# Pooled attention and a top-1 mixture of experts on one core: the last pair's sums earlier, the routings' products and the first expert's weight pieces in other places, the gates on ScalarE

## The chip, the core and the metric

The kernel runs on one core of a Trainium2 chip. Five engines work beside each other, each on its own queue in order: TensorE (PE; its weight loads are listed as PEld), VectorE (DVE), ScalarE (ACT), GpSimd (POOL) and SyncE (SP), which here only issues transfers. The metric is the device time of one execution in microseconds. About 2% is what a measurement of this kernel can tell from no change.

## The reference

K and V are averaged over 8 neighbouring rows, softmax attention is taken over the 72 pooled rows, and each of the 4608 resulting rows of 512 goes to one of 8 experts, the one with the largest logit.

```python
k_p = k.reshape(B, H, Sp, pool, D).mean(axis=3)      # B = H = 8, S = 576, D = 64, Sp = 72
v_p = v.reshape(B, H, Sp, pool, D).mean(axis=3)
attn = softmax(scale * q @ k_p.T)
x = (attn @ v_p).transpose(0, 2, 1, 3).reshape(4608, 512)
expert_idx, gate_w = argmax(x @ w_gate), softmax(x @ w_gate)[expert_idx]
# each expert takes its rows in order, up to capacity (1152); rows beyond it give zero
h = np.maximum(np.einsum('ecd,edf->ecf', disp, w1), 0.0)   # F = 1024
y = np.einsum('ecf,efd->ecd', h, w2)
out[i] = gate_w[i] * y[expert_idx[i], pos[i]]
```

## The kernel before

Attention runs over 36 *units*. A unit is 256 rows of one batch for four heads, and each odd batch is led by a unit for the last 64 rows of two batches. The main loop (`for n in range(nu + 2)`, from L1022) works on unit n's scores (`score`, PE writes ps), its row maxima and differences on VectorE (`softmax`: mx at L486, pt at L491), and its exponentials on ScalarE (`exp`, L494), while PE transposes unit n-2 (`p_t`, pp, copied to pT by ScalarE at L503), multiplies it by the pooled V (`av`, pa, L516) and VectorE normalises it (`norm`: rz, reciprocal, xo, lt, L525 to L542). There is one tile pa, so PE's next `av` waits until `norm` has read it, that is until lt. `q_part` transposes the next unit's queries (pq), which ScalarE copies to qT (L463). Small products and transposes share two PSUM banks in turn (`bank`).

Around this stand queues of small pieces, taken a few at a time by `step`: gq (GpSimd's sums for pooling, `tree`: three additions a third, L370 to L374; later the pieces of w1), rq (the routings), dq (the masks) and sq (scatters of routed rows to `slots`, L679, each behind a small write of the tile `apart`). `load_kv` brings the raw K and V of a pair of batches, `pool` sums them: that of the fourth pair (batches 6 and 7) is put on the queue at the end of unit 14, behind a copy that waits for unit 14's mx.

A *routing* (`route`) is a chain of some 18 VectorE operations on the logits of two batches: gmx, gd, gme, gmm, the one-hot rows oh, their running sums su, the counts (L628), then on PE the products po, and behind them gps (a sum, and a product with oh), gpos, ghi, gix and pairs. Each `yield` in it is one step. It stands in rq from units 10, 19 and 28 on, and for batch 6 from 32; `step(rq)` is called once in `softmax`, three times in `norm` and once ahead of `norm`, there with 4 steps, or 8 in the last eight units. `favourite` finds from the second routing which expert leads, and its w1 is loaded (L816) and split into two halves of precision in eight pieces (`split_early`): ScalarE copies w1h (L125), GpSimd subtracts w1l (L126).

After attention a loop runs over tiles of 256 rows of one expert. PE makes the hidden rows (ph, three banks, L150), ScalarE takes relu into hh (L1129), VectorE the rest into hl (L1130), PE multiplies by w2 (y, L159). Where the expert changes (`sw`), ScalarE and VectorE split w1 and w2 (w2h at L125, w2l at L126). `gate` scales y into ys (L1152), GpSimd scatters ys and rows of zeros to the output (L100) and gathers the next rows (xg, L95). Ahead of a pass each engine loads registers from the table cf (L1159 to L1165).

Of the kernel before, what the change touches and what calls it, by code (L numbers as in the profile page):

```python
# [10 lines left out]
F32 = mybir.dt.float32  # L11
# [20 lines left out]
def pooled_attn_top1_moe(ctx: ExitStack, tc: tile.TileContext, q, k, v, wg, w1, w2, cap, out):  # L32
# [7 lines left out]
    nc = tc.nc  # L40
# [121 lines left out]
    with ExitStack() as actx:  # L162
# [421 lines left out]
        def route(bp, t0, G, blk, tail, prods, sc, count=False, run=None):  # L584
# [43 lines left out]
                    nc.vector.tensor_reduce(out=cum[-1], in_=oh[:, NB : 4 * NB + 2].bitcast(F32).rearrange("p f e -> p e f"), axis=AX.X, op=ALU.add)  # L628
                yield
            if gn > 3:  # L630
                yield
                yield
                yield
            po = bank([P, 512], "po")[:, 0 : 4 * E].rearrange("p (a e) -> p a e", a=4)
            prods = [x for x in prods if before or x[1] != "c"]
            for n_, (w, x, l, m) in enumerate(prods):
# [98 lines left out]
        def drain(q_):  # L735
            while q_:
                step(q_)

        with tc.manual_schedule():
# [17 lines left out]
            def ahead(b):  # L757

                if b + 1 < B:
                    load_q(b + 1)  # L760
                if b % 2 == 0:
                    load_qtail(b)
                if b == LAST - 1:
                    dq.append(masks)

            nu = len(units)
# [238 lines left out]
            def hooks(n):  # L1005

                p, j = divmod(n, NPU)
                if n == 0:
                    red(vps[0][:, NR - 1 :], raws[0][1][2][:, 2:3])
                    pooled(1)  # L1010
                    pool(1)
                if p == B // 2:
                    return
                if p + 2 < B // 2:
                    if j == (4 if p == 0 else 2):
                        load_kv(p + 2)
                    if j == (7 if p == 0 else 5):
                        if p:
                            nc.gpsimd.tensor_copy(apart, early["mx"][:, 0, 0:1])
                        pooled(p + 2)  # L1020
                        pool(p + 2)
                if n == 3 * NB:  # L1022
                    drain(gq)
                    gq.append(setup_rest())
                    drain(gq)
                    setup_rows()

            for n in range(nu + 2):
                u = units[n] if n < nu else None
                p = units[n - 2] if n > 1 else None  # L1030
                nx = units[n + 1] if n + 1 < nu else None
                new = n and u and u.b != units[n - 1].b
                if new:
                    assert not aq
                    ahead(u.b)
                if n == n_start:
                    start_weights()
                if n == n_early:
                    start_early()
                if n == n_early + 1:  # L1040
                    drain(gq)
                    split_early(0, 2 * KD, nc.gpsimd)
                if n == n_early + 3:
                    start_ids()
                if n == n_early + 4:
                    start_rows()
                if u:
                    u.score(0)
                if p:
                    p.p_t(0)  # L1050
                if u:
                    u.score(1)
                    u.softmax()
                step(aq)
                if p:
                    p.p_t(1)
                if n == nu + 1:
                    for c in range(KF):
                        nc.scalar.copy(wr["h"][:, c], wr[2][:, c])
                if n >= nu:  # L1060
                    hidden(0, n - nu)
                if nx:
                    nx.q_part()
                flush()
                step(aq)
                if n == 1:
                    busy(5)
                    hq.append(prep_v(0))
                    step(hq)
                if u:  # L1070
                    u.exp()
                if p:
                    p.open()
                    p.av(0)
                turns(n)
                if p:
                    p.av(1)
                step(rq, 4 if NPU < n < nu - 8 else 8 if n >= nu - 8 else 0)
                step(dq)
                if p:  # L1080
                    p.norm()
                    r = route_of(p)
                    if r:
                        rq.append(r)
                        if p.b == early_b - 1:
                            rq.append(favourite())
                hooks(n)
                step(gq, 4 if n <= n_early else 0 if n_early + 3 <= n < n_early + 5 else 2)
                step(sq, 2 if n < nu - 10 else 4)
                step(aq)  # L1090
            flush()
# [4 lines left out]
    with ExitStack() as bctx:  # L1096
# [52 lines left out]
                split(hh[s], hl[s], p)  # L1149

        def gate(i):
            nc.vector.tensor_scalar_mul(ys[i], y[i], io[:, i, 1:2].bitcast(F32))  # L1152

        nc.sync.dma_start(xs[NT : NT + 1, :], zrow[0:1])
        nt = nc.values_load(ntl[0:1, 0:1], min_val=E, max_val=MT // 2 + E)
# [1 line left out]
        with tc.For_i(0, nt, 1, iteration_sync="reg_based") as t:  # L1157
            with tc.manual_schedule():
# [24 lines left out]
                load_w1(we, cond=nw > 0, bounds_check="skip_entire_dma")  # L1183
                columns(io[:, :, 1], ids[:, ds(ct, 2), 1])
                masked(io[:, :, 0], ct, mkeep)
                gate(1)
                masked(iz, cd, mdrop)
                nc.gpsimd.tensor_sub(guard[:, 0], iz, iz)
                for i in range(2):
                    scatter(iz[:, i : i + 1], zrow[:, :], across_iterations=True)  # L1190
                gate(0)
                with tc.If(sw > 0):
                    split_w2()
                load_w2(we, cond=nw > 0, bounds_check="skip_entire_dma")
                for i in (1, 0):
                    nc.gpsimd.tensor_sub(guardf, ys[i][:, 0:2], ys[i][:, 0:2])
# [27 lines left out]
```

## Time and profile before

| | us |
|---|---|
| median of 3 runs | 640.29 (633.51 to 642.54) |
| the profiled execution | 639.53 |
| its span, first to last instruction | 637.5 |
| PE busy in it | 614.1 (96%) |
| DVE, ACT, POOL busy | 332.5, 236.3, 297.4 |
| mean granted PE clock | 0.987 |

The views of the profile that are read below: busy time and clock by stretch, the waits summed by pair, the timeline of one engine, and the chain of work that ended last. In a timeline a row gives the start and the length in us, the engine, the line of the program, the operation, out<-in, the form, the count, and in brackets how long the engine was idle before and what ended that. Units begin on PE at 64.27 (unit 11), 68.72 (12), 75.13 (13), 108.95 (21), 145.45 (28), 150.17 (29), 162.87 (31) and 179.07 (34).

### The profile page before, as it was taken

How to read it: one execution, taken by the hardware profiler on the slowest of the kernel's cores; microseconds unless marked ns; L12 is line 12 of the kernel's file. 1: busy time of each engine (PE TensorE's matmuls, PEld its weight loads, DVE VectorE, ACT ScalarE, POOL GpSimd, SP SyncE). 2: the span in 40 equal slices, each digit the busy share in tenths (PEclk: the TensorE clock that was granted, in tenths of full speed). 3: DMA queues.
4: the chain of work that ended last, by engine and by line, in shares of the span. 5: the costliest groups of instructions: out<-in, count | busy, mean ns of one | idle time of the engine just before them, and what ended most of it. 6: DMA issues, size and time to landing. Idle time of an engine off the chain costs nothing.

```text
span 637.5 us, 14824 instructions
## 1 busy us (share of the span) xinstructions
PE 614.1 (96%) x4249; PEld 554.1 (87%) x4250; DVE 332.5 (52%) x720; ACT 236.3 (37%) x403; POOL 297.4 (47%) x468
## 2 busy tenths in 40 slices
PE   9899999899999999999899999999999999999994
PEld 8889899798889889988789989988899888989983
DVE  4667868777788322268447731326422585323222
ACT  2555576366544211157245511117111472111111
POOL 7799499253743422424435522434434145441344
PEclk9999999799999999999999999999999999999997
DMA  9989953283191610228728640213612181210112
GB/s 325 359 330 323 349 183 122 72 258 101 53 329 53 230 35 33 66 81 309 241 82 308 230 141 33 66 33 120 235 47 66 41 282 36 66 51 19 62 49 66
DMA packets 47084, 93.81 MB, mean 147 GB/s; under 512 B 13392, under 2 KB 23632, under 8 KB 47060
## 3 DMA queue, kind: packets, MB, share of 16 engines
q1 hardware_dynamic: 30836, 60.37, 27.6%
q0 software_dynamic: 11392, 21.57, 11.3%
q10 hardware_dynamic: 4832, 11.56, 4.8%
q8 instruction: 14, 0.23, 0.1%
q14 instruction: 10, 0.08, 0.0%
HBM read 132.97 MB, written 31.27 MB: 258 GB/s over the span
## 4 chain that ended last, share of the span: by engine, by line
PE 60%; DVEq 2%; issue 2%; DVE 1%; POOL 1%; ACT 0%; POOLq 0%; ACTq 0%
PE y L159 30%; PE ph L150 23%; PE ph L1140 4%; PE px L1117 2%; PE ph L1147 1%; DVE w2l L126 0%; POOL out_dram L100 0%; DVE hl L1130 0%; DVEq L1165 0%; DVEq L1164 0%; DVEq L1163 0%; ACT w2h L125 0%; DVEq L1160 0%; DVEq L1159 0%; POOL xg L95 0%
## 5 line engine op out<-in xcount | busy, mean ns | idle before, releaser
L1129 ACT ACTIVATE hh<-ph 128x512 fp32r<-128x512 f32 x60 | 35.8, 598 | 170.1 <-PE ph L150 170.0
L1130 DVE SCALAR_TENSOR_TENSOR hl<-ph,hh 128x512 fp32r<-128x512 f32 x60 | 40.7, 690 | 109.4 <-ACT hh L1129 62.5
L150 PE MATMUL ph<-xh,w1h 128*128 128x256 f32 x480 | 76.5, 282 | 4.6 <-DVE hl L1130 3.9
L150 PE MATMUL ph<-xh,w1l 128*128 128x256 f32 x480 | 75.9, 281 | 0.0
L150 PE MATMUL ph<-xl,w1h 128*128 128x256 f32 x480 | 75.9, 281 | 0.0
L150 PEld LDWEIGHTS ph<-xh,w1h 128*128 128x128 f32 x480 | 65.8, 189 | 6.9 <-DVE hl L1130 4.8
L159 PE MATMUL y<-w2h,hh 128*128 128x512 f32 x280 | 71.7, 398 | 0.0
L95 POOL DMA_INDIRECT xg<-xs,ix x42 | 43.5, 1035 | 58.2 <-PE y L159 50.0
L516 PE MATMUL pa<-vbd,pT 96*128 96x146 f32 (+1 forms) x480 | 67.1, 296 | 3.5 <-DVE lt L542 3.5
L159 PE MATMUL y<-w2h,hl 128*128 128x512 f32 x280 | 69.3, 390 | 0.0
L159 PE MATMUL y<-w2l,hh 128*128 128x512 f32 x280 | 69.2, 389 | 0.0
L150 PEld LDWEIGHTS ph<-xl,w1h 128*128 128x128 f32 x480 | 65.2, 190 | 0.0
L150 PEld LDWEIGHTS ph<-xh,w1l 128*128 128x128 f32 x480 | 64.7, 189 | 0.0
L516 PEld LDWEIGHTS pa<-vbd,pT 96*128 96x128 f32 (+1 forms) x480 | 57.1, 181 | 6.8 <-DVE lt L542 4.5
L159 PEld LDWEIGHTS y<-w2l,hh 128*128 128x128 f32 x280 | 52.6, 188 | 11.1
L159 PEld LDWEIGHTS y<-w2h,hl 128*128 128x128 f32 x280 | 52.6, 188 | 10.9
L100 POOL DMA_INDIRECT out_dram<-zrow,iz x40 | 51.3, 1282 | 16.9 <-issue 14.9
L159 PEld LDWEIGHTS y<-w2h,hh 128*128 128x128 f32 x280 | 49.6, 188 | 9.6 <-ACT hh L125 0.9
L126 DVE TENSOR_TENSOR xl<-px,xh 128x512 fp32r<-128x512 f32 x40 | 25.8, 686 | 60.9 <-ACT xh L125 60.9
L93 POOL TENSOR_TENSOR guard<-ix 128x2 int32<-128x2 int32 x21 | 4.0, 193 | 101.5 <-DVE ix L90 96.8
L503 ACT COPY pT<-pp 96x384 f32<-96x384 f32 x72 | 33.8, 474 | 45.0 <-PE pp L502 44.4
L679 POOL DMA_INDIRECT slots<-pairs,gix x36 | 35.4, 983 | 30.3 <-DVE pairs L672 13.0
(236 smaller groups left out, 1051.8 us busy)
## 6 DMA issues: line engine op xcount, KB each, us to landing
r<-in_moe_w_dram SPq DMA_DIRECT2D x84, 1024.0 KB, 11.1
raw<-in_k_dram SPq DMA_DIRECT2D x12, 768.0 KB, 6.5
raw<-in_v_dram SPq DMA_DIRECT2D x12, 768.0 KB, 10.6
xs<-xo ACTq DMA_DIRECT2D x16, 512.0 KB, 3.1
qblk<-in_q_dram SPq DMA_DIRECT2D x14, 512.0 KB, 7.7
raw<-in_moe_w_dram SPq DMA_DIRECT2D x4, 512.0 KB, 4.8
r<-in_moe_w_dram ACTq DMA_DIRECT2D x2, 1024.0 KB, 6.9
qblk<-in_q_dram SPq DMA_DIRECT2D x4, 256.0 KB, 8.3
```

Source lines behind the costliest of these rows:

```text
L95: nc.gpsimd.indirect_dma_start(out=dst[:, i, :].bitcast(F32), out_offset=None, in_=src, in_offset=bass.IndirectOffsetOnAxis(ap=ix[:, i, 0: ...
L100: ins = nc.gpsimd.indirect_dma_start(out=out[:, :], out_offset=bass.IndirectOffsetOnAxis(ap=i_, axis=0), in_=src, in_offset=None, bounds_c ...
L126: eng.tensor_sub(lo, src, hi.bitcast(F32))
L150: nc.tensor.matmul(p[:, f2], a[:, c, f * P : (f + 1) * P], b[:, c], start=(f2 == 0 and j == 0 and c == 0), stop=(f2 == 1 and j == 2 and c ...
L159: nc.tensor.matmul(y, a[:, c, i * P : (i + 1) * P], b[:, c], start=(n == 0), stop=(n == 3 * KF - 1))
L503: nc.scalar.copy(self.pT[:, j], pp[0:KC, 0:HC])
L516: nc.tensor.matmul(self.pa[us, j, h0 * XW : (h0 + 2) * XW], self.pT[:, j, c, us], vbd[b % 2][:, cc].rearrange("r a x -> r (a x)"), start=( ...
L679: ins = nc.gpsimd.indirect_dma_start(out=slots[:, :], out_offset=bass.IndirectOffsetOnAxis(ap=ix[:, g, 0:1], axis=0), in_=pairs[:, pr + g0 ...
L1117: nc.tensor.transpose(px[i][:, c], xg[:, i, c * P : (c + 1) * P], identr)
L1129: nc.scalar.activation(hh[s], p, AF.Relu)
L1130: nc.vector.scalar_tensor_tensor(out=hl[s], in0=p, scalar=0.0, in1=hh[s].bitcast(F32), op0=ALU.max, op1=ALU.subtract)
L1140: nc.tensor.matmul(ph[f], a[:, c, r], b[:, c, fs], start=(j == 0 and c == 0), stop=(j == 2 and c == KD - 1))
```

## The change

Six edits:

- In `route`, the chains of more than three tiles take 5 (with counts) or 7 (without) empty steps ahead of the products po, where there were 3.
- `step(rq)` ahead of `norm` takes 8 steps in all units below 14 (before: 4 from unit 10 on), then 4, and 8 in the last eight as before.
- The fourth pair's sums are put on the queue at the end of unit 12 instead of unit 14, behind a copy that waits for unit 12's mx; three steps of gq follow in that unit, so one K sum stands ahead of the first scatters.
- The eight pieces of w1 are taken 2, 3, 3 at units 26, 27 and 28 (before: 2, 2 at 26 and 27, and 2, 2 at 30 and 31); the additional ones stand behind `p_t(0)` and `p_t(1)`.
- The masks are made at unit 22 instead of 27.
- `gate` is an ACTIVATE on ScalarE with a scale from io, and both gates stand behind the split of w2.

```diff
             if gn > 3:
-                yield
-                yield
-                yield
+                for _ in range(5 if count else 7):
+                    yield
...
-                if b == LAST - 1:
+                if b == LAST - 2:
                     dq.append(masks)
...
-                    if j == (7 if p == 0 else 5):
-                        if p:
-                            nc.gpsimd.tensor_copy(apart, early["mx"][:, 0, 0:1])
+                    if p == 0 and j == 7:
                         pooled(p + 2)
                         pool(p + 2)
                 if n == 3 * NB:
...
+                    nc.gpsimd.tensor_copy(apart, early["mx"][:, 0, 0:1])
                     setup_rows()
+                    pooled(3)
+                    pool(3)
...
+                more = 1 if n_early + 1 < n < n_early + 4 else 0
                 if u:
                     u.score(0)
                 if p:
                     p.p_t(0)
+                step(gq, more)
...
                 if p:
                     p.p_t(1)
+                step(gq, more)
...
-                step(rq, 4 if NPU < n < nu - 8 else 8 if n >= nu - 8 else 0)
+                step(rq, 8 if n < 2 * NPU - 4 or n >= nu - 8 else 4)
...
-                step(gq, 4 if n <= n_early else 0 if n_early + 3 <= n < n_early + 5 else 2)
+                step(gq, 3 if n == 3 * NB else 4 if n <= n_early else 2 if n == n_early + 1 else 1)
...
         def gate(i):
-            nc.vector.tensor_scalar_mul(ys[i], y[i], io[:, i, 1:2].bitcast(F32))
+            nc.scalar.activation(ys[i], y[i], AF.Copy, scale=io[:, i, 1:2].bitcast(F32))
...
-                gate(1)
                 masked(iz, cd, mdrop)
...
-                gate(0)
                 with tc.If(sw > 0):
                     split_w2()
+                for i in (1, 0):
+                    gate(i)
```

On GpSimd, behind the last piece of `setup_rest` (rmi, unit 12), the order before is this; slots are the scatters, t and kp the tiles of a sum:

```order
L335 IOTA rmi_187 32x64
L678 MEMSET apart_184 128x1
L679 DMA slots_64<-pairs_66,gix_1120 36864x2
L678 MEMSET apart_184 128x1
L679 DMA slots_64<-pairs_66,gix_1120 36864x2
L1019 COPY apart_184<-mx_1168 128x1
L370 TENSOR_TENSOR t1_1211<-raw_1001 128x768
```

and in the changed kernel:

```order
L335 IOTA rmi_187 32x64
L1023 COPY apart_184<-mx_1026 128x1
L370 TENSOR_TENSOR t1_1106<-raw_1001 128x768
L372 TENSOR_TENSOR t2_1107<-t1_1106 128x384
L374 TENSOR_TENSOR kp_1104<-t2_1107 128x192
L677 MEMSET apart_184 128x1
L678 DMA slots_64<-pairs_66,gix_1080 36864x2
```

The copy waits for unit 12's mx instead of unit 14's, and the first K sum moved ahead of the first two scatters.

On VectorE, in the same unit 12, behind PE's products po of the first routing, there stood before:

```order
L644 TENSOR_TENSOR gps<-su,po 128x64
L646 SCALAR_TENSOR_TENSOR gps<-po,oh_180 128x8
L655 TENSOR_TENSOR gps<-gps,oh_180 128x64
L525 TENSOR_SCALAR rz<-pa 128x8
L658 TENSOR_REDUCE gpos<-gps 128x9
L527 RECIPROCAL rz<-rz 128x8
L662 TENSOR_SCALAR ghi<-gpos 128x9
L541 TENSOR_TENSOR xo<-pa,rz 128x2x256
L542 TENSOR_TENSOR lt<-pa,rz 128x2x32
```

and now stands:

```order
L643 TENSOR_TENSOR gps<-su,po 128x64
L645 SCALAR_TENSOR_TENSOR gps<-po,oh_180 128x8
L654 TENSOR_TENSOR gps<-gps,oh_180 128x64
L657 TENSOR_REDUCE gpos<-gps 128x9
L661 TENSOR_SCALAR ghi<-gpos 128x9
L663 TENSOR_SCALAR ghi<-ghi 128x9
L664 SCALAR_TENSOR_TENSOR gpos<-gpos,gmm 128x9
L667 TENSOR_REDUCE gse<-ex_183 128x9
L669 SCALAR_TENSOR_TENSOR gix<-ghi,gpos 128x9
L671 RECIPROCAL pairs<-gse 128x9
L525 TENSOR_SCALAR rz<-pa 128x8
```

The rest of the chain moved ahead of the normalisation rz, xo, lt of unit 10.

On ScalarE, from the exponential of unit 27 to the first pT of unit 29, there stood before (in the changed kernel the two pieces ahead of the exponential of unit 27 come on top):

```order
L494 ACTIVATE pt<-pt 128x576
L125 CAST w1h<-raw 128x512 x2
L503 COPY pT<-pp 96x384 x2
L463 COPY qT<-pq 128x512
L494 ACTIVATE pt<-pt 128x576
L417 COPY kbs_147<-pk 64x64x5
```

and now stands:

```order
L494 ACTIVATE pt<-pt 128x576
L125 CAST w1h<-raw 128x512
L503 COPY pT<-pp 96x384
L125 CAST w1h<-raw 128x512
L503 COPY pT<-pp 96x384
L125 CAST w1h<-raw 128x512
L463 COPY qT<-pq 128x512
L494 ACTIVATE pt<-pt 128x576
L417 COPY kbs_147<-pk 64x64x5
L417 COPY kbs_147<-pk 64x64x4
L417 COPY kbs_147<-pk 64x64x5
L417 COPY kbs_147<-pk 64x64x4
```

Pieces of w1 (w1h) moved between the copies pT, and one more, the eighth, follows these kbs copies ahead of unit 29's first pT.

## Rows read from the trace of the kernel before

**Rows 1.** Busy time and granted clock (PEclk) by stretch, us.

```profile
105.00:135.00 30.00, 27.86 (x218) 24.78 (x217) 24.23 (x74) 15.19 (x31) 13.92 (x20) 0.89 0.45 158
150.00:165.00 15.00, 14.29 (x111) 12.83 (x110) 10.73 (x33) 7.84 (x17) 4.27 (x5) 0.89 0.24 72
```

**Rows 2.** Timeline of PE: waits at the routings, and places named.

```profile
71.39 1.02 PE L516 MATMUL pa<-vbd,pT 96*128 96x146 f32 x6 [0.41 <-DVE lt L542]
...
77.68 1.66 PE L516 MATMUL pa<-vbd,pT 96*128 96x146 f32 x12
...
113.34 1.01 PE L516 MATMUL pa<-vbd,pT 96*128 96x146 f32 x6 [2.13 <-DVE lt L542]
...
147.53 0.66 PE L462 MATMUL pq<-identr,qblk 128*128 128x128 f32 x4 [0.28 <-ACT pT L503]
...
155.28 0.28 PE L641 MATMUL po<-su,matr 128*128 128x16 f32 x1 [0.71 <-DVE su L621]
...
166.34 1.01 PE L516 MATMUL pa<-vbd,pT 96*128 96x146 f32 x6 [0.75 <-DVE lt L542]
...
178.94 0.27 PE L641 MATMUL po<-su,matr 128*128 128x8 f32 x1 [1.19 <-DVE su L621]
...
184.38 1.74 PE L516 MATMUL pa<-vbd,pT 96*128 96x146 f32 x12
```

**Rows 3.** Timeline of DVE: second routing (two rows) and third.

```profile
107.83 1.59 DVE L598 TENSOR_TENSOR gd<-lg,gmx 128x72 f32<-128x72 f32 x1
...
109.98 1.69 DVE L614 TENSOR_TENSOR oh<-cw,gmm 128x64 fp32r<-128x64 f32 x1
...
153.49 0.22 DVE L598 TENSOR_TENSOR gd<-lg,gmx 128x72 f32<-128x72 f32 x1
```

**Rows 4.** Timeline of POOL: fourth pair's sums, first and last tree.

```profile
82.56 1.83 POOL L370 TENSOR_TENSOR t<-raw 128x768 f32<-128x768 f32 x1
...
107.51 1.81 POOL L370 TENSOR_TENSOR t<-raw 128x768 f32<-128x768 f32 x1
```

**Rows 5.** Timeline of DVE: units 11 and 12, and a routing's chain undivided.

```profile
71.26 0.34 DVE L628 TENSOR_REDUCE oh<-oh 128x8 fp32r<-128x112 f32 x1
71.52 0.75 DVE L486 TENSOR_REDUCE mx<-ps 128x8 f32<-128x576 f32 x1
...
75.49 0.22 DVE L655 TENSOR_TENSOR gps<-gps,oh 128x64 f32<-128x64 f32 x1
...
76.73 0.21 DVE L542 TENSOR_TENSOR lt<-pa,rz 128x64 f32<-128x64 f32 x1
...
197.69 0.17 DVE L644 TENSOR_TENSOR gps<-su,po 128x16 f32<-128x16 f32 x1 [0.92 <-PE po L641]
...
198.89 0.18 DVE L672 RECIPROCAL pairs<-gse 128x3 f32<-128x3 f32 x1
```

**Rows 6.** Timelines of DVE, POOL and ACT: ghi, pieces of w1, copies kbs.

```profile
163.32 1.11 DVE L662 TENSOR_SCALAR ghi<-gpos 128x9 f32<-128x9 f32 x1
...
161.88 2.49 POOL L126 TENSOR_TENSOR w1l<-raw,w1h 128x512 fp32r<-128x512 f32 x2 [9.83 <-ACT w1h L125]
...
145.98 1.12 ACT L125 CAST w1h<-raw 128x512 fp32r<-128x512 f32 x2
...
149.44 1.72 ACT L417 COPY kbs<-pk 64x320 f32<-64x320 f32 x4
```

**Rows 7.** PE's waits summed; ACT's timeline; the chain that ended last.

```profile
PE ph L150 <- DVE hl L1130: 3.9, 4, 1.8
...
524.81 2.00 ACT L125 CAST w2h<-r 128x1024 fp32r<-128x1024 f32 x2 [0.55 <-DMA r<-in_moe_w_dram]
...
239.07 11.31 PE ph L150 x96
...
526.93 0.07 DVEq L1192
...
531.17 0.70 DVE hl L1130
```

## The prediction

> **What bounds the kernel.** I read the busy time and granted clock by stage first, then TensorE's waits, then the orders of the engines around each wait. TensorE (PE) works almost without a pause, so a term counts only where PE waits, or works at the lower clock, and where nothing else comes to wait there instead. In the attention stage such places lie at the four routings. [...] Behind the third routing PE waits 0.75 us (unit 31), behind the fourth 1.19 us (unit 33) [rows 2]. In the expert loop the only waits that repeat are those for hl where an expert changes: 3.9 us in four places [rows 7].
>
> **Second routing (sums moved to unit 12).** The wait of 2.13 us comes from VectorE: gd took 1.59 us and oh 1.69 us there, where the same gd of the third routing took 0.22 us [rows 3]. gd ended at 109.42; GpSimd's first step of the last V sum, begun at 107.51 and 1.81 us long, ended at 109.32 [rows 3, 4]. So these operations, which read two SBUF operands, stood until GpSimd's sum was through. The fourth pair's sums ran from 82.56 to the tree begun at 107.51 [rows 4]. Now they are issued behind unit 12's mx, which begins at 71.52 and takes 0.75 us [rows 5]: a start at 72.6, 10 us sooner. Even with two more slot scatters between them they are over well ahead of 107. gd and oh then take some 0.2 us, lt ends about 0.4 us before PE needs it, and PE waits for nothing: -2.13 us. If the fall of the clock hangs on that wait, 3.3 us come back too: together -5.4.
>
> **First routing (eight steps a unit instead of four; K sum beside it).** What was spread over units 11 to 13 now stands ahead of two normalisations. In unit 11 the counts (0.34 us, L628) move ahead of lt [rows 5], and PE already waited 0.41 us for that lt at 71.39 [rows 2]: +0.35. In unit 12 everything from gpos to pairs moves ahead of rz. A whole such chain, with nothing between, took from 197.69 to 198.89 plus 0.18 [rows 5]; its part behind gps and the product is 0.95 us. The K sum's last step overlaps its start: begun at 72.6, its steps of 1.83 us [rows 4] and, at half and a quarter of the size, about 1.0 and 0.6 us end near 76.3, and the product, at 75.49 before [rows 5], would be due at 75.9; I add 0.3 us. lt, at 76.73 plus 0.21 before, ends at 76.94 + 0.35 + 0.95 + 0.3 = 78.55, and PE's pa of unit 13, begun at 77.68 before [rows 2], is due at 78.05: a new wait of 0.5, with the hand-over 0.65. Below, the chain meets no sum (+0.3); above, one operation stands behind a whole first step of 1.83 us (+2.2). I take +1.0 for both units, since the scatters behind the K sum wait for pairs themselves and so keep GpSimd's next sum out of the chain.
>
> **Third routing (sums later, w1 pieces sooner).** The po products now stand a unit later, when su is long done: -0.71, and with the clock -1.65. ghi of this routing took 1.11 us beside a w1l piece [rows 6]; all pieces are through by then, so of PE's 0.75 us about 0.25 stays (the chain is still ahead of rz): -0.5.
>
> **w1 pieces.** ScalarE has 0.56 us for each (two in 1.12) [rows 6]. Units 27 and 28 now hold three each, and the eighth follows the kbs copies of unit 28, which took from 149.44 to 151.16 without a pause [rows 6]. Unit 27 has room. In unit 28 three pieces (1.7 us) meet the 1.72 us of kbs on ScalarE, beside two pT, qT and exp. PE's wait of 0.28 us at 147.53, for a pT behind two pieces [rows 2], goes; but kbs now begins a piece (0.56) later, less what PE no longer waits: about 0.35, for which PE's second pp of unit 29 waits. pq of that unit waits for a pT behind the eighth piece, 0.56 and the hand-over: about 0.7. With 0.1 in unit 28 the sum is +0.9 (estimates); bounds -0.28 (hidden) and +1.7 (three pieces in full). GpSimd's halves of the pieces run on to about the same point of unit 29 and may hold gd there, but VectorE has to wait for PE's pa afterwards in any case.
>
> **Fourth routing.** PE's 1.19 us for su goes, since po moves behind unit 34. But then the chain from gps to pairs (1.2 us) lies ahead of unit 34's rz, with po (0.35 us on PE) ahead of it: lt comes some 1.45 us later, and PE, which did not wait for it at its next pa at 184.38 [rows 2], 0.35 later: a new wait of at most 1.1; I take 0.95, as lt was a little ahead. Net -0.24; bounds -1.19 and +0.3.
>
> **Masks and gates.** The masks, some 0.75 us of VectorE work, move to unit 22, where they delay lt to about when PE needs it: 0, at most their own time of under 1 us. The gates leave VectorE. At a change of expert, though, it is not VectorE's data that comes last: the last w2h copy ends at 524.81 + 2.00 = 526.81, VectorE's sequencer passes L1192 at 526.93, and after 4.2 us of register loads hl begins at 531.17 [rows 7]. The gates now stand behind that copy on ScalarE, so it ends no sooner, and hl with it: 0. If w2l were the limit, up to 3.9 us would come back. In the other passes PE has no wait to lose.
>
> **Sum.** +1.0 - 5.43 - 2.36 - 0.5 + 0.9 - 0.24 = -6.6 us. Against the profiled execution, 639.5 us, that is 632.9 us; the median shown, 640.3, lies 0.8 above it, and the fastest run shown (633.5) may be one in which the clock fell less often, so the gain in medians may be smaller.
>
> **A rule weighed.** The rows show the clock at half after waits of 2.13 and 0.71 us between spells of work, and not after the waits of 0.75 and 1.19 us at 166 and 178 us [rows 1, 2]. So what the clock does behind a wait is not fixed by the wait's length, and the 5 us are the least certain term. [...]
>
> **Rivals.**
> 1. *The clock falls all the same*, behind the new waits in units 12, 13 and 29. The waits saved count, the 4.95 us do not: 632.9 + 4.95 = 637.8. For it: 0.71 us was enough once. Against: each new wait is small, and the waits of 0.75 and 1.19 us left the clock alone. Chance 0.17.
> 2. *The low clock does not hang on the two waits at all* and stays where it was: 637.8 again, with no new wait needed. For it: two longer or equal waits left the clock alone; against it: both low stretches begin right behind a wait. Chance 0.05. [...]
> 3. *The sums still stand in gd's way*, because K's raw data or the scatters' wait for pairs holds GpSimd's chain up by more than some 4 us. Then the second routing gives nothing: 632.9 + 5.4 = 638.3. Against it: the data are loaded from unit 11 on, ahead of use. Chance 0.08.
> 4. *The gates were on the path*: the four hl waits go: 632.9 - 3.9 = 629.0. Against it stand the 0.12 us from the last w2h copy to L1192. Chance 0.07.
> 5. *Slower*: ScalarE now waits for a pass's last product before it can load the next pass's registers. hh, then hl, must free the first ph bank before PE's fourth group, 8.5 us after that product (three quarters of the 11.3 us of its 96 products [rows 7]). If gate, loads and relu take more than 7.2 us, each microsecond above is lost in each of some 12 passes; at 8.2 us the time is 632.9 + 12 = 645. VectorE's five loads take 4.2 us [rows 7], ScalarE has two, so it should be ready in about 3. Chance 0.05.
>
> **Chances and range.** My forecast has 0.54, the rivals in their order 0.17, 0.05, 0.08, 0.07 and 0.05; 0.04 is left for what I don't see. The forecast's own range, from its bounds, is 630.5 to 635.5. Taking in rivals 1 to 4 gives 628 to 639, which leaves out about 0.15. About 2% is what a measurement of this kernel can tell from no change: 627.5 or less has 0.03, 653 or more 0.02, so within 2% has 0.95.
>
> **What the new profile would show.** Right: no PE wait near unit 21 and gd, oh at about 0.2 us; granted clock near 1 from 100 to 160 us; no wait of po for su; waits of PE for lt in units 12, 13 and 35 of 0.5 to 1 us and for ScalarE in unit 29; the hl waits at changes of expert unchanged. Wrong: a clock of 0.89 or less in these stretches, gd still over 1 us, new PE waits above 2 us, or hl waits that are gone.

## The result, and the profile after

The changed kernel took 631.2 us in the median of 11 runs (630.5 to 634.5), the kernel before 639.0 us (11 runs) on the same chip: a ratio of 0.9889, 95% interval 0.9863 to 0.9915. The prediction was 632.9 us. On another chip, later, the same two kernels stood level: 0.9993 (0.9968 to 1.0017). Both belong to the result; the experiments say where the gain went, and only in part why. Whether it is the chip or the hour that makes the difference is not shown.

The profiled execution of the changed kernel is its slowest one: 634.5 us, span 631.8. Busy time and clock by stretch (the columns are those of [rows 1], and so are the last two stretches; the first had a clock of 1.00 in the kernel before, whose row is put ahead):

```profile
70.00:85.00 15.00, 14.59 (x127) 13.16 (x125) 11.95 (x37) 8.58 (x18) 5.64 (x14) 1.00 0.87 315
```

```profile
70.00:85.00 15.00, 14.16 (x98) 12.42 (x97) 10.53 (x33) 5.16 (x12) 9.34 (x15) 0.77 0.80 297
...
105.00:135.00 30.00, 29.89 (x260) 26.84 (x259) 24.18 (x84) 19.14 (x39) 10.83 (x20) 1.00 0.45 156
...
150.00:165.00 15.00, 14.23 (x123) 12.88 (x124) 11.38 (x36) 7.91 (x17) 6.89 (x12) 1.00 0.81 291
```

The two low stretches are gone, and a new one stands at 70 to 85 us: 0.77 over 15 us, that is about 3.4 us of work lost to the lower clock ("us of clock" below). Timeline of PE, to be read against [rows 2]. In the brackets, `issue` means that the trace shows nothing that the engine waited for, `remote` that it was released by something that the trace does not name:

```profile
71.58 1.02 PE L516 MATMUL pa<-vbd,pT 96*128 96x146 f32 x6 [0.83 <-DVE lt L542]
...
150.52 0.65 PE L462 MATMUL pq<-identr,qblk 128*128 128x128 f32 x4 [0.61 <-ACT pT L503]
...
161.96 1.01 PE L516 MATMUL pa<-vbd,pT 96*128 96x146 f32 x6 [0.25 <-DVE lt L542]
...
180.46 1.73 PE L516 MATMUL pa<-vbd,pT 96*128 96x146 f32 x12 [1.12 <-DVE lt L542]
```

No wait of 0.2 us or more is left in unit 21 and none for su; the new ones in units 12, 29 and 35 and the small rest in unit 31 are there. VectorE's operations of the second routing and of the third (against [rows 3, 6]) run free of GpSimd, in 0.17 to 0.23 us:

```profile
111.20 0.22 DVE L598 TENSOR_TENSOR gd<-lg,gmx 128x72 f32<-128x72 f32 x1
...
111.99 0.23 DVE L614 TENSOR_TENSOR oh<-cw,gmm 128x64 fp32r<-128x64 f32 x1
...
159.88 0.17 DVE L661 TENSOR_SCALAR ghi<-gpos 128x9 f32<-128x9 f32 x1
```

The expert loop gained too, which was not forecast. PE's waits, summed (us, times, longest; against [rows 7]):

```profile
PE pa L516 <- DVE lt L542: 2.9, 6, 1.1
PE ph L150 <- DVE hl L1133: 1.6, 4, 0.6
```

From its first product (PE at 216.30 before, at 212.81 after) to the end of the span the loop took 421.2 us before and 419.0 after. The waits for hl at four changes of expert fell from 3.9 us (1.84, 0.70, 0.45, 0.95) to 1.6 (0.56, 0.44, 0.27, 0.32). ScalarE's last two copies of w2 at the first change, before and then after, and VectorE's work behind them after:

```profile
300.68 2.00 ACT L125 CAST w2h<-r 128x1024 fp32r<-128x1024 f32 x2 [1.43 <-DMA r<-in_moe_w_dram]
```

```profile
293.80 4.13 ACT L125 CAST w2h<-r 128x1024 fp32r<-128x1024 f32 x4
```

```profile
296.60 4.63 DVE L126 TENSOR_TENSOR w2l<-r,w2h 128x1024 fp32r<-128x1024 f32 x4 [0.17 <-issue]
302.34 1.89 DVE L1133 SCALAR_TENSOR_TENSOR hl<-ph,hh 128x512 fp32r<-128x512 f32 x3 [1.10 <-issue]
```

And the load that the copies of before waited for, on SP's queue, before and then after:

```profile
288.15 2.70 SPq L122 DMA_DIRECT2D r<-in_moe_w_dram  x2
```

```profile
283.93 2.70 SPq L122 DMA_DIRECT2D r<-in_moe_w_dram  x2
```

It goes out 4.2 us earlier where the loop began only 3.5 us earlier, so 0.7 us sooner within its pass. The copies no longer wait for the weights, and hl now follows w2l by VectorE's own issue. Of the 2.3 us gained in these waits, 1.9 lie at the two changes (the first and the last) whose copy had waited for a load.

### The profile page after: what moved, and what is told of

Read it like the earlier page. It is cut to its first block, busy times and chain, and to the rows that moved or that the text cites. A ratio compares the mean times of both kernels' runs of the same rounds, so it can differ in the third digit from the quotient of the medians.

```text
span 631.8 us, 14919 instructions
## 1 busy us (share of the span) xinstructions
PE 612.6 (97%) x4249; PEld 552.1 (87%) x4250; DVE 302.5 (48%) x680; ACT 261.6 (41%) x443; POOL 301.4 (48%) x468
## 5 line engine op out<-in xcount | busy, mean ns | idle before, releaser
L95 POOL DMA_INDIRECT xg<-xs,ix x42 | 46.7, 1111 | 57.6 <-PE y L159 49.8
L100 POOL DMA_INDIRECT out_dram<-zrow,iz x40 | 49.3, 1234 | 15.8 <-issue 15.8
L125 ACT CAST xh<-px 128x512 fp32r<-128x512 f32 x40 | 21.5, 589 | 73.9 <-PE px L1120 73.5
```

The lines of the kernel that those rows point to most:

```text
L95: nc.gpsimd.indirect_dma_start(out=dst[:, i, :].bitcast(F32), out_offset=None, in_=src, in_offset=bass.IndirectOffsetOnAxis(ap=ix[:, i, 0: ...
L100: ins = nc.gpsimd.indirect_dma_start(out=out[:, :], out_offset=bass.IndirectOffsetOnAxis(ap=i_, axis=0), in_=src, in_offset=None, bounds_c ...
L125: nc.scalar.copy(hi, src)
```

## The experiments

All twelve are set against the kernel before on the same chip. The first four ran on a second chip (kernel before 643.3 us), the next four on a third (642.2), the last four on a fourth (642.7).

| kernel | median us | ratio to before | 95% interval |
|---|---|---|---|
| gates alone | 641.8 | 0.9976 | 0.9959 to 0.9992 |
| sums alone | 642.6 | 0.9991 | 0.9973 to 1.0009 |
| changed, steps of the first routing as before | 640.2 | 0.9952 | 0.9932 to 0.9973 |
| changed, gates on VectorE behind w2l | 645.7 | 1.0043 | 1.0020 to 1.0066 |
| changed, again | 642.1 | 0.9993 | 0.9968 to 1.0017 |
| changed, w2's load held back | 639.9 | 0.9985 | 0.9961 to 1.0008 |
| changed, register loads later | 645.9 | 1.0063 | 1.0039 to 1.0087 |
| four edits on top of the changed kernel | 642.3 | 1.0012 | 0.9988 to 1.0035 |
| changed, w1's pieces as before | 636.3 | 0.9924 | 0.9893 to 0.9954 |
| w1's pieces alone | 654.7 | 1.0199 | 1.0166 to 1.0231 |
| changed, w1's pieces and steps as before | 635.1 | 0.9899 | 0.9870 to 0.9928 |
| changed, 24 small copies first on ScalarE | 641.2 | 0.9997 | 0.9966 to 1.0028 |

All but w1's pieces alone lie within 2%; what is told apart below rests on the intervals and on rows of the traces. Times are compared on one chip only, and a trace is a single execution.

### The gates

```diff
+            nc.scalar.activation(ys[i], y[i], AF.Copy, scale=io[:, i, 1:2].bitcast(F32))
-                gate(1)          # ahead of masked(iz ...)
-                gate(0)          # ahead of split_w2()
+                for i in (1, 0):
+                    gate(i)      # behind split_w2()
```

> The kernel before with the gates moved to ScalarE and nothing else. Theory (a chain over the weights: with no gates ahead of it VectorE's w2l of the first change of a pair starts sooner, SP's load of the next w2 goes out about 0.8 us sooner relative to the pass, and the w2h copies of the second change no longer wait for it): the waits of PE for hl fall from 3.9 to about 1.6 us, ScalarE's waits of 1.43 and 0.55 us for r<-in_moe_w_dram go, time 2.3 us under the kernel before, 636.7. Rival 1 (prediction's step: the gates are not on the path): hl waits 3.9, time 639.0. Rival 2 (the loop gained in the changed kernel only since its attention part ended at another moment): 639.0 as well, with the DMA waits still there. Clock in the attention part as before: 0.89 in 105 to 135 us.

Measured: 0.9976, a gain of 1.5 us (0.5 to 2.6); the loop, from its first product to the end of the span, took 421.8 us against 424.1 in the kernel with the sums alone, whose gates stand on VectorE as before. The hl waits:

```profile
PE ph L150 <- DVE hl L1130: 1.3, 3, 0.7
```

The sum by name misleads here, since the trace puts some of these waits to `issue`. Taken by place, PE waits 1.6 us at the four changes in gates alone and 2.5 us in sums alone; ahead of two products y it waits another 1.1 us for hh in gates alone and 2.4 in sums alone:

```profile
PE y L159 <- ACT hh L125: 2.4, 2, 1.2
```

So the gates were on the path, and alone they bring what the loop of the changed kernel gained (2.3 us here, 2.2 there). On this chip no copy w2h waits for a load in either kernel, though: the chain over the late load, seen on the first chip, is not the whole cause. The next kernel put the gates on VectorE, behind w2l:

```diff
-            nc.scalar.activation(ys[i], y[i], AF.Copy, scale=io[:, i, 1:2].bitcast(F32))
+            nc.vector.tensor_scalar_mul(ys[i], y[i], io[:, i, 1:2].bitcast(F32))
```

> The changed kernel with the gates on VectorE, but behind w2l and not ahead of it. It holds the two accounts of the gates apart. Theory (what counted was that w2l, and with it the next load of w2, went out late): ScalarE's copies w2h wait for no DMA, as with the gates on ScalarE; the two gates of 0.75 us lie behind w2l, under VectorE's register loads or ahead of them, so hl comes 0 to 1.5 us later at each of four changes: hl waits 1.6 to 7.6 us, 631.2 to 637.2. Rival (VectorE's own time alone counted, not the load): the waits of 1.43 and 0.55 us for r<-in_moe_w_dram are back, and hl waits of 3.9 us or more.

Measured: 1.0043, the loop 423.7 us, as long as with the gates at their old places. One of PE's waits now names the gate itself:

```profile
PE ph L150 <- DVE hl L1133: 1.2, 2, 0.7
PE ph L150 <- DVE ys L1155: 1.2, 1, 1.2
```

By place PE waits 3.1 us at the four changes. What counts is that two gates (0.75 us each) stand in VectorE's order between a pass's end and the next pass's hl; ahead of w2l and behind it cost the same. The load's part could not be told apart here, since no copy waited for it on this chip in any of the kernels.

### The register loads

```diff
-                ct = ...; c2 = ...; cd = ...   # three values_load on VectorE at the top of the pass
+                c2 = ...; ct = ...; cd = ...   # behind hidden_all / hidden_one
```

> The changed kernel with VectorE's three register loads of the columns (ct, c2, cd) behind the pass's last hl instead of ahead of its first. Theory (with the gates gone, hl at a change of expert waits for VectorE's chain of five register loads, 4.2 us from the end of w2l's issue): hl waits 1.6 to under 0.3 us, 1.3 us under the changed kernel. Rival (hl waits for the end of w2l itself): hl waits unchanged at 1.6, same time.

Measured: 1.0063. The waits for hl are gone, as the theory said, but another took their place, and the loop took 425.4 us against 421.5:

```profile
PE ph L150 <- DVE xl L126: 3.2, 4, 0.9
```

The loads now delay ix (2.83 us behind the last hl where it stood 0.53 behind, at about 540 us), and with it the gather and xl. They are cheapest where they stood.

### The sums

```diff
                 if n == 3 * NB:
+                    nc.gpsimd.tensor_copy(apart, early["mx"][:, 0, 0:1])
                     setup_rows()
+                    pooled(3)
+                    pool(3)
```

> The kernel before with the fourth pair's pooled sums moved to unit 12, behind one K sum, and nothing else. Theory (GpSimd's sums held gd and oh, and the fall of the clock hangs on the wait of 2.13 us): no wait of PE in unit 21, gd and oh about 0.2 us each, granted clock about 1 from 105 to 135 us, time -5.4: 633.6. Rival 1 (the low clock does not hang on the wait): wait gone but clock still 0.89 there, -2.1: 636.9. Rival 2 (the sums still in gd's way): gd over 1 us, 639.0. In all of them the waits for su (0.71, 1.19) and the hl waits (3.9) stay, and the clock of 150 to 165 us stays low.

Measured: 0.9991. The mechanism in unit 21 was right, and no gain came of it. Timelines of DVE, POOL and PE:

```profile
75.92 1.43 DVE L662 TENSOR_SCALAR ghi<-gpos 128x9 f32<-128x9 f32 x1
...
79.51 1.34 DVE L670 SCALAR_TENSOR_TENSOR gix<-ghi,gpos 128x9 int32<-128x9 f32 x1
...
109.84 0.22 DVE L598 TENSOR_TENSOR gd<-lg,gmx 128x72 f32<-128x72 f32 x1
```

```profile
75.50 1.82 POOL L370 TENSOR_TENSOR t<-raw 128x768 f32<-128x768 f32 x1
...
79.01 1.81 POOL L370 TENSOR_TENSOR t<-raw 128x768 f32<-128x768 f32 x1
```

```profile
78.12 1.76 PE L516 MATMUL pa<-vbd,pT 96*128 96x146 f32 x12 [0.76 <-DVE lt L542]
...
128.79 0.53 PE L502 MATMUL pp<-identr,pt 128*96 128x128 f32 x3 [1.80 <-ACT kbs L417]
```

gd of the second routing takes 0.22 us and unit 21 waits for nothing. But the first routing's chain meets the sums now: ghi ends 0.03 us after one GpSimd step, gix 0.03 us after another, and lt is late. With a wait of 1.13 us for ScalarE at 82.65 us (not shown) and the 1.80 us above, behind which the clock fell again (0.94 from 105 to 135 us), nothing is left of the 5.4 us. The clock fell once more behind PE's wait of 1.19 us for su near 178 us (0.91 from 165 to 185 us). The first routing's waits are the sums' doing. The 1.80 us is not shown to be: w1's pieces alone, with the sums where they were, wait 2.00 us at the same place, and gates alone does not.

### The steps of the first routing

```diff
-                step(rq, 8 if n < 2 * NPU - 4 or n >= nu - 8 else 4)
+                step(rq, 4 if NPU < n < nu - 8 else 8 if n >= nu - 8 else 0)
```

> The changed kernel with four steps of the first routing in a unit, as before, instead of eight. Theory (the eight steps delay lt in unit 12 and that is what the clock fell behind): PE's wait for lt in unit 12 goes back from 0.83 to about 0.41 us, unit 13 waits for nothing, the clock is about 1 from 70 to 80 us; 630.2 by the waits alone (1.0 under the changed kernel's median of 631.2), and up to 3 us less in those executions in which the clock fell there. Rival (the first routing costs nothing in the usual execution): 631.2.

Measured: 0.9952, with no wait of PE shown in units 12 and 13. The five pauses that the change puts ahead of the products are enough: with four steps a unit they place gpos, ghi and gix behind lt, where a stretched operation (gix took 0.53 us) cost no wait. It also lost time elsewhere, to a standstill of ScalarE (3.81 us, then 3.16 us more in the same profile) that is told of next. How it stands to the changed kernel can't be read across chips; the pair on the fourth chip below can.

### The changed kernel again, and where it lost its gain

> The changed kernel itself once more, beside the three below, since the runs of the first four kernels stood at 643.3 us for the kernel before where 639.0 had been measured ahead of them. Theory A (ScalarE stalls in units 31 to 33 because the load of w2, which now starts behind the last piece of w1 at 151 us instead of 173 us, fills the DMA engines just there, and whether it stalls differs from chip to chip): ratio to the kernel before 0.993 to 0.997, with waits of PE of 1.6 to 2.4 us near 165 and 170 us and a half clock behind them. Theory B (the stall belongs to the four edited kernels alone): ratio 0.989 as measured first, and no such wait.

Measured: 0.9993; theory A's numbers. Between 165 and 185 us, where the first chip showed a clock of 1.00, stands now:

```profile
165.00:185.00 20.00, 17.31 (x99) 15.39 (x100) 10.01 (x30) 6.68 (x13) 4.83 (x10) 0.66 0.31 94
```

That is 6.8 us of clock. The first engine to stop was ScalarE; its timeline, then PE's:

```profile
167.04 0.47 ACT L503 COPY pT<-pp 96x384 f32<-96x384 f32 x1 [3.03 <-issue]
```

```profile
167.57 0.54 PE L846 MATMUL pxe<-identr,xg 128*128 128x128 f32 x4 [1.44 <-issue]
...
169.88 1.33 PE L479 MATMUL ps<-kbs,qT 128*128 128x144 f32 x4 [0.46 <-issue]
...
173.47 0.87 PE L502 MATMUL pp<-identr,pt 128*96 128x128 f32 x3 [0.67 <-DVE xl L126]
```

The copy pT waits for PE alone, and its product pp was through at about 164.5; yet ScalarE stood still until 167.04, and PE, whose next product pxe takes its turn in the banks behind that copy, with it. On the first chip ScalarE idled 0.84 us ahead of the same copy. All seven kernels here that have the whole change's order of w1's pieces stood still in unit 32 (162 to 172 us, for 2.7 to 3.8 us), and so did w1's pieces alone (3.74 us, in its unit 32). Of those with the old order, the gates alone and the sums alone, stood still near 189 us for 1.64 and 1.81 us; PE waited 0.71 and 1.43 us there, and the clock held at 1.00. ScalarE was not always alone in it: VectorE stood still for 2.73 us (`remote`) beside it in w1's pieces alone.

One thing that the prediction had not seen was the first suspect. With the pieces of w1 done sooner, SP's load of w2 starts at 151 us, not at 173, and the DMA engines are 0.81 busy from 150 to 165 us in the first profile of the changed kernel, for 0.24 in [rows 1]. I held it back:

```diff
+                for c in (0, 4):
+                    nc.vector.memset(wr[2][:, c, 0:1], 0.0)
                 load_w2(early["e0"])
```

> The changed kernel with a write of one column into each half of w2's buffer on VectorE in unit 33, for which the load of w2 must wait, so that it starts at about 172 us again as before the change. Theory A (the early load of w2 is what stalls ScalarE in units 31 to 33): no wait of PE over 0.4 us between 160 and 172 us, granted clock 1 in 165 to 190 us, ScalarE's stall gone or back at its place near 189 us with 1.6 us; 3 to 6 us under the changed kernel where that one stalls (both on this chip), and no difference where it does not. Theory B (the stall has nothing to do with the load): the same waits of 2 us, and the time of the changed kernel.

Measured: 0.9985, the same as the changed kernel within the intervals. SP's load, then ScalarE and the stretch ahead of it:

```profile
175.14 1.04 SPq L122 DMA_DIRECT2D r<-in_moe_w_dram  x2
```

```profile
172.20 0.58 ACT L125 CAST xh<-pxe 128x512 fp32r<-128x512 f32 x1 [3.05 <-remote]
```

```profile
155.00:175.00 20.00, 14.51 (x118) 12.34 (x118) 10.83 (x32) 6.93 (x15) 9.79 (x18) 0.98 0.08 28
```

The load starts at 175.14 us, the DMA engines are 0.08 busy from 155 to 175 us, and ScalarE stands still all the same. Theory A falls: the early load is not the cause. A kernel with four edits at once (steps as before, five pauses in every routing, w2 held back, loads behind hl) gained nothing either:

> The changed kernel with four steps of the first routing in a unit, five pauses ahead of the products in every routing (so that the third and the fourth pair of chains are divided between two units), w2's load held back to unit 33, and the three register loads behind hl. By the waits: no wait in units 12 and 13 (-1.0), hl (-1.3), the wait of 1.1 us in unit 35 halved (-0.5), no stall in units 31 to 33 and no fall of the clock behind it: 2.8 us under the changed kernel where it does not stall, 6 to 9 us where it does. Rival: the divided chains bring new waits for lt in units 30 to 35, and it stands level with the kernel that holds w2 back alone.

Measured: 1.0012. It held the harmful loads (its loop took 425.0 us) and stood still in both places; what its pauses alone do stays untold:

```profile
165.05 0.47 ACT L503 COPY pT<-pp 96x384 f32<-96x384 f32 x1 [2.76 <-issue]
...
188.38 0.85 ACT L503 COPY pT<-pp 96x384 f32<-96x384 f32 x2 [2.34 <-remote]
```

The next suspect was ScalarE's own program: a place where its instructions run out.

```diff
         nc.scalar.copy(identr, mats[:, 0])
+        for _ in range(24):
+            nc.scalar.copy(junk, mats[:, 0, 0:1])
```

> The changed kernel with 24 copies of one column put ahead of ScalarE's first work, where it idles 8.6 us, and nothing else. It asks whether ScalarE's standstill belongs to a place in its program by the count of its instructions. Theory F (it waits for its instructions, and the place where they run out is fixed by their count): the standstill moves 24 instructions ahead, to about unit 29 (150 us), and is gone from 164 to 172 us. Theory G (it belongs to something that other engines or the DMA do at that time): it stays at unit 32, near 167 us. The time alone does not tell them apart: 0 to 2 us over the changed kernel by the copies.

Measured: 0.9997, and the standstill did not move:

```profile
168.16 0.47 ACT L506 COPY pT<-pp 96x384 f32<-96x384 f32 x1 [3.02 <-issue]
```

Twelve of the 24 copies ran where ScalarE idled, the others between its next copies, all of them by 18.2 us and so far ahead of unit 32. Theory F falls, so far as 24 instructions reach; G, that other engines or the DMA have a hand in it, is the theory left of the two, and no run names what it would be. That the trace calls several of these waits `remote` leaves a third open: a signal that came late.

### The pieces of w1

```diff
-                more = 1 if n_early + 1 < n < n_early + 4 else 0
-                step(gq, more)       # twice, between VectorE's parts
```

> The changed kernel with the pieces of w1 at their old places in ScalarE's order. In the runs of the changed kernel on the second and third chip ScalarE stood still for about 3 us at a pT of unit 32 (167 us), with no cause named, and the clock fell behind it; in two kernels that leave the pieces where they were it stood for 1.6 to 1.8 us at a pT near 189 us instead. Theory P (the order of the pieces puts ScalarE's standstill to where TensorE waits for it): no wait of PE over 0.5 us between 163 and 172 us, a standstill near 185 to 190 us, clock 1 from 165 to 185 us, ratio to the kernel before 0.988 to 0.993. Theory Q (the standstill is not tied to the pieces): the waits near 167 us as in the changed kernel, ratio 0.996 to 1.000.

Measured: 0.9924, the ratio that theory P said, and ScalarE has no idle time over 0.92 us there that the trace leaves unnamed. Not all of P's signs came: PE waited 1.32 us for lt at 163.26, where P had nothing over 0.5, and 1.57 us for a pT at 177.87, ahead of which ScalarE was idle 2.05 us; the trace puts that to PE's pp, although both its pp are recorded as over by 176.30. In this execution the clock fell behind two waits, at the first routing (3.4 us of clock) and behind this pT (1.8). PE, and the two stretches:

```profile
71.69 1.02 PE L516 MATMUL pa<-vbd,pT 96*128 96x146 f32 x6 [1.10 <-DVE lt L542]
...
177.87 0.66 PE L462 MATMUL pq<-identr,qblk 128*128 128x128 f32 x4 [1.57 <-ACT pT L503]
```

```profile
70.00:85.00 15.00, 13.90 (x96) 12.16 (x95) 10.55 (x33) 5.13 (x11) 9.81 (x19) 0.77 0.82 308
...
165.00:185.00 20.00, 17.31 (x132) 15.45 (x131) 14.18 (x44) 10.18 (x20) 11.57 (x19) 0.91 0.72 239
```

Its executions differ in the clock: five lasted 635.6 to 636.4 us at a mean clock of 0.992 to 0.996, three 639.2 to 640.2 us at 0.985 to 0.989.

The other way round, the pieces alone:

> The kernel before with the pieces of w1 moved and nothing else. Theory P: ScalarE's standstill of about 3 us at unit 32 with waits of PE of 1.4 to 2.4 us and half a clock behind it: 1.5 to 9 us slower than the kernel before, ratio 1.002 to 1.014. Theory Q: +0.9 us by the prediction's term (waits of 0.6 in unit 29), ratio 1.001, and a standstill near 189 us as in the other kernels made from the kernel before.

Measured: 1.0199, 12.0 us slower, beyond both theories. More than half of it is not the standstill. Timelines of DVE, POOL, PE and ACT, and a stretch:

```profile
143.94 6.09 DVE L346 TENSOR_SCALAR mkeep<-spos,capf 128x288 int32<-128x288 f32 x1
```

```profile
143.70 6.15 POOL L126 TENSOR_TENSOR w1l<-raw,w1h 128x512 fp32r<-128x512 f32 x5
```

```profile
151.55 1.83 PE L516 MATMUL pa<-vbd,pT 96*128 96x146 f32 x6 [5.34 <-DVE lt L542]
```

```profile
150.00:160.00 10.00, 8.45 (x47) 7.65 (x48) 6.42 (x20) 4.87 (x10) 2.98 (x4) 0.66 0.08 14
```

```profile
178.87 0.47 ACT L503 COPY pT<-pp 96x384 f32<-96x384 f32 x1 [3.74 <-remote]
```

The mask mkeep, 0.37 us in all other kernels, lasted 6.09 us beside five pieces w1l on GpSimd and ended 0.18 us after them; PE waited 5.34 us, and the clock cost 3.4 more. The edit that makes the masks at unit 22 takes them out of the pieces' way: in every kernel with both edits mkeep took 0.37 us. The standstill of 3.74 us comes behind it: PE waited 2.80 us for it, and the clock, 0.66 from 175 to 185 us, cost another 3.4.

Last, without the pieces and without the eight steps:

> The changed kernel with w1's pieces at their old places and four steps of the first routing in a unit. By theory P and the waits it should stand best of all: no waits in units 12, 13 and 29, no standstill at unit 32: 1 us under the one with eight steps, ratio to the kernel before 0.986 to 0.992. By theory Q 0.995 to 1.000.

Measured: 0.9899, 635.1 us, the best here, and the only one of the fourteen traces without a fall of the clock ahead of the end: 1.3 us under the kernel with eight steps on the same chip, and all its executions within 1.3 us of each other. PE's wait of 0.41 us in unit 12 is that of the kernel before (theory P had none), and it still waits 1.32 us for lt at 160.03 and 1.49 for the pT at 174.57, with the clock at 1.00. PE at the first routing, and the same stretches:

```profile
71.53 1.02 PE L516 MATMUL pa<-vbd,pT 96*128 96x146 f32 x6 [0.41 <-DVE lt L542]
```

```profile
70.00:85.00 15.00, 14.59 (x126) 13.14 (x126) 12.46 (x37) 8.53 (x18) 12.80 (x22) 1.00 0.84 310
...
165.00:185.00 20.00, 17.19 (x149) 15.91 (x147) 15.51 (x50) 9.12 (x19) 11.23 (x21) 1.00 0.83 276
```

## Why the prediction was right, and where its steps were not

**Second routing (-5.4): right.** gd and oh at 0.22 us, the wait gone, the clock 1.00. The 3.3 us, and the 1.65 of the third routing, are the share missing from the mean clock in [rows 1], 0.11 of 30 and of 15 us; in the same trace the granted clock is 0.50 of full speed from 117 to 121 us, behind the wait of 2.13 us that ends at 113.34, and 0.50 from 158 to 160 us, behind the 0.71 us that end at 155.28. In sums alone the fall came back behind another wait, of 1.80 us, in the same stretch. In the fourteen traces the clock falls 18 times between the first units and the end of the work, each time during a wait of PE or within some 3 us behind one, which leaves nothing to rival 2, a clock that hangs on no wait; but a wait does not always bring a fall (last section), so the 3.3 us were likely and not certain. Rival 3 fell with gd at 0.22.

**Third and fourth routing (-2.36, -0.5, -0.24): right on the first chip.** po waits no more, unit 31 waits 0.25 us as forecast, unit 35 1.12 for 0.95. That the waits of 0.75 and 1.19 us had left the clock alone is right, but rows 1 end at 165 us; the stretch behind, in the kernel before, is this:

```profile
165.00:185.00 20.00, 17.36 (x149) 15.82 (x148) 16.38 (x51) 11.23 (x22) 14.09 (x23) 1.00 0.59 197
```

**First routing (+1.0): the waits were sized right or too high, the clock was not counted.** Unit 12 waits 0.83 us, 0.42 more than before for the 0.35 forecast, and the chain met no sum; the hand-over from lt to PE, put at 0.15 us in the forecast for unit 13, was the author's estimate, and in the trace of before it is 0.06 (lt over at 113.28, pa from 113.34); unit 13 was forecast to wait 0.65 and shows at most 0.33 (the changed kernel again). But in the profiled execution the clock fell there, for 3.4 us: rival 1 at one of its three places. 634.5 less 3.4 is 631.1, the median, and the mean clock of the others is 0.992 to 0.996 where this one has 0.991; so in the usual execution the fall did not come. Eight steps instead of four cost 1.3 us on the fourth chip, in the median, where three executions of the kernel with eight steps show the lower clock.

**w1's pieces (+0.9): within its bounds on the first chip (0.6 in unit 29, 0.28 gained: +0.3), wrong on the others.** The step failed by what it left out. On the fourth chip the pieces' new places cost 636.3 against 641.2 us for the changed kernel with its 24 copies: about 5 us (the 24 copies themselves are taken to cost little: the qT behind the last of them began at 18.34 us, in the changed kernel's first trace at 18.11). What goes with them, ScalarE's standstill and the clock's fall behind it, is in no row of before, nor in the first chip's; its own cause stays open.

**Masks (0): right, but for a reason not given.** 0 was the price of moving them; not to move them cost w1's pieces alone 5.3 us and the clock behind. The prediction looked for the pieces at gd, not at the masks.

**Gates (0): wrong; rival 4 was half right.** The step that failed reads "VectorE's sequencer passes L1192 at 526.93" 0.12 us after the last w2h copy, and takes the copy for the cause. A few rows ahead in the same chain stands the gate itself, and w2l behind it (so too at 300.80; at the other two changes the chain names the copy):

```profile
525.80 0.09 DVE ys L1152
...
526.47 0.40 DVE w2l L126
```

At two of the four changes that copy had itself waited for a load (1.43 and 0.55 us), which waits for the w2l of the change ahead, which stood behind the gates: whoever frees w2l frees the copy as well. And at every one of the four changes w2l followed the second gate without a pause. One place of four was read. The gain was 2.2 us, not rival 4's 3.9, since the register loads remain.

**The sum: right on the first chip.** Forecast -6.6 against the profiled execution of before; with the gates' unforeseen -2.2 that makes -8.8. Measured between the two profiled executions: -5.0 (639.5 to 634.5), or -8.4 without the 3.4 us of clock that the usual execution doesn't lose. Between the medians it is -7.8. That the profiled execution came within 1.6 us of the forecast is partly luck: -2.2 and +3.4, neither of them forecast, stand against each other. On the other chips the forecast is off, on the fourth by about what w1's pieces cost there. Rival 5, ScalarE late for each pass, has no trace.

## What to carry to other kernels

When a wait ends on two things at once, follow each one back a whole pass before you call the other harmless: a late copy may wait for a load that waits for the very work you want to move. Edits that put GpSimd's work beside VectorE's come in sets: the sums needed the pauses, the pieces the earlier masks, and each alone was level (0.9991) or slower (1.0199). And a gain of 1% wants a second chip: one edit of this change cost almost nothing on one, and on the others most of the gain went with it.

## What was not expected of the hardware

**VectorE waited through a run of GpSimd's instructions.** mkeep, with one tensor operand, stood from GpSimd's first piece to its fifth, 6.1 us in w1's pieces alone. These pieces followed each other without a pause (five of 1.25 us or more in 6.15); ghi of sums alone got in behind a single step, with 0.07 us to the next. In the traces gd (before), ghi and gix (sums alone) end 0.10, 0.03 and 0.03 us after a GpSimd step, and for mkeep the wait went over five instructions in a row. Which operations wait so, and why, no run shows: xo of sums alone, at 77.26 us, took 0.68 us beside such a step, as long as it takes elsewhere (0.69).

**The clock behind short waits.** It fell behind 0.83 us (the changed kernel, first chip) and 1.10 (w1's pieces as before), and stayed at 1.00 behind 1.08 us at the same place in the changed kernel again. Near 128 us it fell behind 1.80 us in sums alone and stayed behind 2.00 in w1's pieces alone:

```profile
127.90 0.53 PE L502 MATMUL pp<-identr,pt 128*96 128x128 f32 x3 [2.00 <-ACT kbs L417]
```

```profile
105.00:135.00 30.00, 26.52 (x228) 23.33 (x227) 23.66 (x74) 15.74 (x33) 15.79 (x23) 1.00 0.46 160
```

Neither the length nor the place of these waits decides it alone, and the mean clock of a kernel's executions differs as if it fell in some and not in others (with w1's pieces as before 0.985 to 0.989 in three, 0.992 to 0.996 in five). A fall cost 1.7 to 6.8 us of clock.

**ScalarE stood still for 1.6 to 3.8 us, with nothing named that it waited for,** in traces from three chips of four. The long ones, 2.7 us or more near unit 32, come with the place of w1's pieces, not with the early load of w2 and not with the count of ScalarE's instructions. In all kernels that have them GpSimd sent nine slot scatters back to back about then (159 to 170 us in the changed kernel again), which the old order divides by two pieces of w1; but on the first chip the same run (161 to 172 us) came with no standstill. The cause stays open.
